# First expert network: low parts of weights and row builds moved to VectorE, sign multiplications to ScalarE

## The chip, the cores and the metric

One core of one Trainium2 chip runs the whole kernel. The metric is device time of one launch in microseconds (us). Five engines run side by side, each through its own list of instructions in order: PE (TensorE, matrix products, with PEld for its weight loads), DVE (VectorE), ACT (ScalarE), POOL (GpSimd, which here also issues all transfers that go by a list of rows) and SP (SyncE, which issues most other transfers). They wait for each other by semaphores.

## The reference

```
X = fft(fft(x, axis=1), axis=2).real          # x: 8 x 3072 x 256
x = X.reshape(N, 256)                         # N tokens
# first network (moe): soft weights
P = exp(x @ w_gate - max)
for _ in range(8):                            # Sinkhorn turns
    P /= P.sum(1) + 1e-9 ; P /= P.sum(0) + 1e-9 ; P *= N / E
for e in range(8):
    out += P[:, e:e+1] * (relu(x @ w1[e]) @ w2[e])      # w1: 256x1024, w2: 1024x256
# second network (moe2): each token goes to its best expert alone
for e in range(8):
    rows = argmax(out @ w_gate2) == e
    out2[rows] = gate_w[rows] * (relu(out[rows] @ u1[e]) @ u2[e])
```

The logits are so far apart that most tokens have one expert with any weight. So the kernel makes lists of (token, expert) pairs, gathers the rows of a list, and runs them in tiles of 128 rows.

## The kernel before

Four phases follow each other: the Fourier transform (0 to about 230 us), the lists of the first network, the first network (272 to 506 us), the lists of the second (`route2`, 506 to 535 us), and the second network (535 to 722 us).

**Tiles.** Each of the 8 experts has three fixed tiles of 128 rows. Six more, the free tiles, go to any expert that has more rows; their weights are gathered by an indirect transfer (`fw`, `rawc`, `gd`) and a free tile runs within an expert from expert 2 on.

**Products.** A float32 product is made as three products of rounded parts (float32r): high by high, low by high, high by low. For this each weight piece is split: ACT copies it to the high part (`w1h`, `w2h`, L826) and `eng` subtracts (L827, 128x1024; L830, 128x32, for eight gate columns that go with a w2 piece). `part(..., i, ...)` with i = 0, 1 are the halves of w1, with i = 2, 3 the halves of w2; in the lists below i = 4, 5 are the two halves of a free tile's w2. The hidden rows are split as well: ACT takes the relu of a PSUM tile (`hh`, L873), DVE makes `hl` from PSUM and `hh` (L434).

**Rows.** A gathered row group `Xg` (128 partitions x 3 tiles x 281) holds a row of the half spectrum; `build` makes from it the group `x` of full rows in four steps: a, the middle column added to and taken from the even part (two operations, 128x99 and 128x96); b, the mirrored part times a sign per row (128x381, `Xg<-Xg,Rsg`); c, a copy of two columns and a sum (128x381); d, a difference (128x381). PE then transposes `x` (L840, or L867 for free tiles), ACT and DVE split it into `xh` and `xl`. Groups 8 and 9 are the rows of the free tiles.

**Sinkhorn.** `sinkhorn` runs the weights of all pairs on DVE while experts 1 to 4 run: logits, `start`, eight turns of ten small DVE operations with one PE product of column sums (L984) between two turns, then `end`, which copies the weights of fixed tiles, one expert at a time, in eight copies (`Rwt<-P`).

**Order.** Nothing is scheduled: each engine's order is that of the code, and `Slots` places side work between the matrix products: slots 0 to 7 after the eight row groups of h, 8 to 10 in the free tile, 11 after the next transposition, 12 to 20 in the fixed tiles. Tables say which slot and which engine: `ONP` lists the (expert, i) whose subtraction POOL makes, `ONB` the experts in which POOL builds the next expert's rows, `FBUILD` the expert, the slots and a flag (1: POOL) for groups 8 and 9. `UPART` has the four slots of expert 7 in which the second network's first weights (u, expert 0) are split, the last two (w2 halves) on POOL. POOL also issues the weighted rows' scatter-adds to `acc` (L803, `acc<-y`), the free tiles' weight gathers, and, once `route2` has the list `Rgidx`, the gathers of the second network's rows (`Xg<-acc,Rgidx`).

```
for s, i, g in ((UPART[0], 0, V), (UPART[1], 1, V), (UPART[2], 2, G), (UPART[3], 3, G)):
    sl.at(E - 1, s, lambda i=i, g=g: part("u", 0, i, g))
on = lambda e: lambda i: G if (e, i) in ONP else V
onb = lambda e: G if e in ONB else V
```

V is VectorE, G is GpSimd. After a second half is split, `part` fetches the next weights into the buffer on SP's queue.

Of the kernel before, what the change touches and what calls it, by code (L numbers as in the profile page):

```python
# [11 lines left out]
AF = mybir.ActivationFunctionType  # L12
ALU = mybir.AluOpType
# [9 lines left out]
def fft_phase(tc, ctx, A, H, Zd, L, rmx, ident, zb, each):  # L23
# [19 lines left out]
    # gate columns in the basis of the transformed rows  # L43
# [16 lines left out]
    def warm(n):  # L60
        """keeps the tensor engine's clock up while it waits."""
        p = pp.tile([128, 512], F32, name="pp")
        for _ in range(n):
            nc.tensor.matmul(p, zb[:, :128], zb, start=True, stop=True)
# [58 lines left out]
    def logits(hd, t0, n, np_):  # L123
# [4 lines left out]
        if t0 % 12 in (0, 4) and n == 4:  # L128
            # rows that are their own mirror count once
            nc.gpsimd.memset(L[0:1, t0 + t0 % 12 // 2, 1], -3e38)  # L130
# [47 lines left out]
    def d_tiles(b, j, ps=None):  # L178
        """third j of the rows of batch b."""
# [11 lines left out]
    # the middle column of all batches  # L191
# [34 lines left out]
    def zero(i):  # L226
        """second batch, while the first is transformed."""
# [66 lines left out]
def _consts():  # L294
# [36 lines left out]
    # rows in turn: columns added, columns subtracted  # L331
# [16 lines left out]
def host_layout(inp):  # L348
# [9 lines left out]
    # rows of the gate, and those of the mirrored columns, in halves  # L358
# [7 lines left out]
NSL = 40                    # row slots per partition  # L366
NS2 = 8                     # rows with more than one live expert
NSA = NSL + 3 * NS2         # pairs: first, second, third and fourth live expert
CAP = 3                     # fixed tiles per expert
NFLAT = 6                   # tiles that any expert may take  # L370
# [3 lines left out]
DG = D + 8                  # a row and its second gate  # L374
DW = DG + 1                 # and its place in the output
# [39 lines left out]
def row_tile(t):  # L415
    """where the rows of a tile lie: after rows of no token come the free tiles."""
    return t + 1 + NFLAT if t < E * CAP else t - E * CAP + 1

# [24 lines left out]
class Route:  # L443
    """lists of rows by expert: one-hot products put every marked slot at its place."""
# [8 lines left out]
    def positions(self, T, M, n, rst, hook=lambda: None, S=None, n1=None):  # L453
        """places of the marked (expert, slot), summed over the experts; 0 for empty slots.
        The caller adds the start of the expert's tiles. Slots from n1 on come first."""
# [25 lines left out]
        # two chains in turn: tiles past the fixed ones, places  # L481
# [16 lines left out]
        if two:  # L498
            # more than a tile of other pairs
# [8 lines left out]
        def later():  # L508
            """experts of the free tiles, rows of their weights, too many tiles."""
# [17 lines left out]
    def split(self, T, gp, cs, n, nm):  # L527
        """tile and row of the places gp + cs; rounding to whole numbers by a large one."""
# [32 lines left out]
def route1(nc, rt, L, rmx, K, R, keep, pool, ring, hooks):  # L561
# [6 lines left out]
    # global maximum  # L568
# [13 lines left out]
    # a key per row: its column and the set of its live experts  # L582
# [19 lines left out]
    # one live expert of every row: the first  # L602
# [15 lines left out]
    # rows with more: their other experts in turn  # L618
# [21 lines left out]
    def during():  # L640
        # while the counts are summed: columns of the slots, first tiles of their experts
# [20 lines left out]
    # the other pairs come first, as they are asked for again  # L662
# [21 lines left out]
    def signs():  # L684
        # sign, whether the pair is the row's first
# [8 lines left out]
        # place of the row's first pair, for its other pairs  # L694
# [17 lines left out]
    def targets():  # L712
        # rows that the other pairs are added to; all else goes to rows of no token
# [23 lines left out]
def route2(nc, rt, lg, K, R, pool, ring, arrive, more, counts, warm):  # L737
# [12 lines left out]
    def choose(a, b):  # L750
        # the first expert with the largest logit
# [35 lines left out]
    # empty places take a row of no token  # L787
# [19 lines left out]
class Moe:  # L807
    """expert networks over tiles of 128 rows; float32 products as three of float32r parts."""
# [6 lines left out]
    def part(self, r, i, eng, g=None):  # L815
        """hi and lo part of a piece; g: eight more columns per row of w2."""
# [16 lines left out]
    def turn(self, xs, hook=None):  # L833
        """transpose tiles into hi and lo parts; hook: rows come tile by tile."""
# [27 lines left out]
    def free_turn(self, xs, x):  # L862
        """transpose the rows of free tiles."""
# [13 lines left out]
    def first(self, W, x, after):  # L877
        """h = relu(x w1), as hi and lo parts."""
# [13 lines left out]
    def gates(self, W, h, n, rows):  # L892
        """second gates of n tiles without their rows; h(m): hi and lo part of rows m."""
# [16 lines left out]
    def second(self, W, h, nd, after=lambda i: None):  # L910
        """h w2 for a tile; h(m): hi and lo part of rows m."""
# [14 lines left out]
    def free_first(self, w, x, i):  # L926
        """the same for a free tile, from whole float32 weights, in three steps."""
# [12 lines left out]
def boltz(nc, o, P, g, bias):  # L940
    """exp(P) as float32 has it, times 2^64: below 2^-126 in steps of 2^-149."""
# [8 lines left out]
def sinkhorn(nc, K, R, pt, pool):  # L950
    """weights of the pairs, in steps: logits of three tiles, turns, end."""
# [21 lines left out]
    def rows(it):  # L973
        o.red(rs, P, ALU.add)
        o.ts(rs, rs, 1e-9 * (2.0 ** 64 if it == 0 else 1.0), ALU.add)
# [15 lines left out]
    def end():  # L991
# [3 lines left out]
        for e in range(E):  # L995
            o.cp(R["wt"][:, e * CAP:(e + 1) * CAP], P[:, e * CAP:(e + 1) * CAP, e])
# [14 lines left out]
def dense(tc, ctx, A, K, rt, R, Ld, H, Pd, out, wg2):  # L1011
    """every row through every expert: any number of live pairs."""
# [43 lines left out]
    def network(w1, w2, xT, wt, acc):  # L1056
        """acc[tok, s] = sum over e of wt[tok, s, e] * relu(x w1) w2."""
# [67 lines left out]
# order in which weights are fetched, and the buffers they take  # L1125
# [4 lines left out]
HOLD = [("u", 0, 1)]        # after it no weights are fetched  # L1130
F0 = 2                      # first expert that a free tile goes with


def run(tc, ctx, A, out, H, acc, Ld, Pd, Gd, Zd):
# [29 lines left out]
    def zeros(n, zt=zt):  # L1164
        """output rows stay zero unless they are written later."""
# [14 lines left out]
    def fetch():  # L1180
        if order:
            s, e, b = order.pop(0)
            if b in "12":
                # room that parts of the first weights do not need yet
# [12 lines left out]
    with tc.manual_schedule():  # L1197
# [27 lines left out]
        with ExitStack() as st:  # L1225
# [7 lines left out]
            def gates2(e, qs=(0, 1)):  # L1233
                """w2 times the second gate."""
# [537 lines left out]
```

## Time and profile before

| | us |
|---|---|
| time, median of 3 runs (775.53 to 784.99) | 777.13 |
| span of the profiled execution, first to last instruction | 722.5 |
| between the two (launch and end, outside the span) | 54.6 |
| PE busy, share of the span | 635.4 (88%) |
| DVE busy | 448.1 (62%) |
| ACT busy | 340.4 (47%) |
| POOL busy | 315.4 (44%) |
| mean granted TensorE clock | 0.943 |

The profiled execution's own device time is not given beside its span; the 54.6 us are taken as outside it. A row of a timeline reads: start, duration, engine, line, operation, output<-inputs, shapes, and in brackets how long the engine was idle before it and what ended that. Durations of one engine's successive instructions overlap by about 0.1 us. A duration runs from the instruction's start to its end, so an instruction that is held up in the middle of its execution shows as a long one, not as an idle engine.

### The profile page before, as it was taken

The page shows a single profiled execution, that of the slowest core. Times are in us where ns is not written, and L with a number is a line of the kernel's source. Part 1 is how long each engine was busy: PE and PEld are TensorE (multiplying, and loading weights), DVE is VectorE, ACT ScalarE, POOL GpSimd, SP SyncE. Part 2 cuts the span into 40 slices and gives each one's busy share as a digit, 9 for nine tenths or more (in the row PEclk, how much of TensorE's full clock was granted, in tenths as well). Part 3 has the DMA queues.
Part 4 walks back from the last instruction along what each step waited for, and adds up shares of the span by engine and source line. Part 5 has one row for each costly group of instructions (what it writes and reads, how often), then busy time and mean ns, then how long its engine had stood idle before and what let it go on. Part 6 is the DMA issues. An engine that isn't in the chain of part 4 may idle for free. (4 is left out here: it accounts for less than half of the span.)

```text
span 722.5 us, 12560 instructions
## 1 busy us (share of the span) xinstructions
PE 635.4 (88%) x4749; PEld 609.5 (84%) x4749; DVE 448.1 (62%) x932; ACT 340.4 (47%) x660; POOL 315.4 (44%) x325
## 2 busy tenths in 40 slices
PE   7888978898998499896969698988499999999996
PEld 4778978898998499895959598987369999999996
DVE  3587456646347967779696946842935567556650
ACT  2455666566754204553344353653215556455651
POOL 2377446645010537839152525424347463422232
PEclk9899999999999859998879899999799999999998
DMA  8989999997769517987543478684727475467410
GB/s 223 241 225 319 325 295 280 301 303 235 258 222 358 205 41 244 197 352 246 159 154 117 151 225 236 184 310 94 250 67 252 169 271 180 164 242 252 168 56 33
DMA packets 67039, 155.43 MB, mean 215 GB/s; under 512 B 17891, under 2 KB 35787, under 8 KB 59164
## 3 DMA queue, kind: packets, MB, share of 16 engines
q1 hardware_dynamic: 56844, 114.83, 50.3%
q0 software_dynamic: 9840, 39.45, 17.3%
q8 instruction: 39, 0.64, 0.4%
q10 hardware_dynamic: 288, 0.27, 0.1%
q14 instruction: 28, 0.23, 0.1%
HBM read 104.00 MB, written 50.44 MB: 214 GB/s over the span
## 5 line engine op out<-in xcount | busy, mean ns | idle before, releaser
L920 PE MATMUL py<-w2l,hh 128*128 128x264 f32 (+1 forms) x480 | 141.5, 295 | 13.8 <-DVE w2l L830 7.8
L920 PE MATMUL py<-w2h,hh 128*128 128x264 f32 (+1 forms) x480 | 143.1, 298 | 0.0
L434 DVE SCALAR_TENSOR_TENSOR hl<-ph,hh 128x384 fp32r<-128x384 f32 (+1 forms) x164 | 85.5, 540 | 92.6 <-ACT hh L873 92.4
L920 PE MATMUL py<-w2h,hl 128*128 128x264 f32 (+1 forms) x480 | 141.2, 294 | 0.0
L920 PEld LDWEIGHTS py<-w2l,hh 128*128 128x128 f32 x480 | 95.9, 200 | 15.1 <-DVE w2l L830 8.4
L873 ACT ACTIVATE hh<-ph 128x384 fp32r<-128x384 f32 (+1 forms) x164 | 76.7, 481 | 53.6 <-PE ph L887 27.6
L150 POOL TENSOR_TENSOR xa<-xa,xm 96x1024 f32<-96x1024 f32 (+1 forms) x30 | 75.3, 2524 | 52.2 <-DMA xm<-in_xm_dram 51.5
L920 PEld LDWEIGHTS py<-w2h,hl 128*128 128x128 f32 x480 | 95.7, 199 | 0.3
L920 PEld LDWEIGHTS py<-w2h,hh 128*128 128x128 f32 x480 | 95.8, 200 | 0.1
L803 POOL DMA_INDIRECT out_dram<-y,Rorow x30 | 32.1, 1070 | 90.0 <-ACT y L1705 39.9
L887 PE MATMUL ph<-xh,w1h 128*128 128x384 f32 x256 | 67.4, 344 | 4.0 <-DVE hl L434 3.9
L73 PEld LDWEIGHTS pp<-ca,w 96*128 96x128 f32 x512 | 60.2, 196 | 6.2 <-DVE w L159 4.2
L73 PE MATMUL pp<-ca,w 96*128 96x96 f32 x512 | 61.8, 280 | 4.1 <-DVE w L159 4.1
L887 PE MATMUL ph<-xl,w1h 128*128 128x384 f32 x256 | 65.2, 336 | 0.0
L887 PE MATMUL ph<-xh,w1l 128*128 128x384 f32 x256 | 65.2, 336 | 0.0
L75 ACT ACTIVATE at<-pp 128x384 f32<-128x384 f32 x64 | 54.0, 847 | 21.1 <-PE pp L73 19.5
L90 PE MATMUL pp<-cb,t 128*128 128x128 f32 x368 | 49.3, 279 | 11.4 <-DVE t L83 11.4
L90 PEld LDWEIGHTS pp<-cb,t 128*128 128x128 f32 x368 | 45.4, 194 | 12.5 <-DVE t L83 12.5
L887 PEld LDWEIGHTS ph<-xh,w1h 128*128 128x128 f32 x256 | 45.0, 188 | 6.6 <-DVE hl L434 5.2
L83 DVE COPY t<-pp 128x512 f32<-128x512 f32 (+2 forms) x56 | 32.4, 608 | 24.6 <-PE pp L81 24.6
L119 DVE COPY hd<-pp 128x281 f32<-128x281 f32 x32 | 14.3, 448 | 53.3 <-ACT hd L121 35.0
L887 PEld LDWEIGHTS ph<-xl,w1h 128*128 128x128 f32 x256 | 46.3, 188 | 0.1
(335 smaller groups left out, 1336.2 us busy)
## 6 DMA issues: line engine op xcount, KB each, us to landing
out_dram<-zt SPq DMA_DIRECT2D x48, 512.0 KB, 3.0
H<-hd SPq DMA_DIRECT2D x24, 562.0 KB, 6.4
xa<-in_xa_dram SPq DMA_DIRECT2D x32, 384.0 KB, 6.1
xm<-in_xm_dram SPq DMA_DIRECT2D x32, 384.0 KB, 8.8
rawa<-in_w_dram SPq DMA_DIRECT2D x8, 1024.0 KB, 6.4
rawb<-in_w_dram SPq DMA_DIRECT2D x8, 1024.0 KB, 8.3
rawa<-in_u_dram SPq DMA_DIRECT2D x8, 1024.0 KB
rawb<-in_u_dram SPq DMA_DIRECT2D x8, 1024.0 KB, 6.1
```

Source lines behind the costliest of these rows:

```text
L73: nc.tensor.matmul(p[:M, i], lhs(4 * h + i), ca, start=True, stop=True)
L75: nc.scalar.activation(out=at[:M, :, :, s0:s0 + 4].rearrange("m g j s -> m s g j"), in_=p[:M], func=AF.Copy)
L83: nc.vector.tensor_copy(out=t[:, :n, :M], in_=p[:, :n, :M])
L90: nc.tensor.matmul(p[:M, i * 128:(i + 1) * 128], t[:, i, :M], cb[:, (g0 + i) * 128:(g0 + i + 1) * 128], start=True, stop=True)
L119: nc.vector.tensor_copy(out=hd, in_=p[:n, :HW])
L150: e.tensor_tensor(out=xa[:, c], in0=xa[:, c], in1=xm[:, c], op=ALU.add)
L434: self.nc.vector.scalar_tensor_tensor(out, a, s, b, op0, op1)
L803: nc.gpsimd.indirect_dma_start(out=dst, out_offset=bass.IndirectOffsetOnAxis(ap=idx, axis=0), in_=src, in_offset=None, **kw)
L873: self.nc.scalar.activation(out=a[:, :n], in_=p[:, :n], func=AF.Relu)
L887: self.nc.tensor.matmul(p[:, :N], w, xx, start=(i == 0), stop=(i == 5))
L920: self.nc.tensor.matmul(p[:, :nd], c, W[2 + m // 4][w][:, m % 4, :nd], start=(m == 0 and i == 0), stop=(m == 7 and i == 2))
```

## The change

Low parts of the first network that POOL subtracted are subtracted by DVE, 14 pieces; POOL's three row builds go to DVE as well (groups of experts 3 and 4, and group 8); the sign multiplication of every build goes to ACT, as three operations of 128x127 with a scale per row in place of one of 128x381; the two w2 pieces of the second network's expert 0 leave slots 15 and 16 of expert 7 and come after `route2` and the gathers' issue, their subtraction on DVE; two small Sinkhorn operations take another form. Transfers of SP keep their order. Comments that were dropped are not shown.

```
-        o.ts(rs, rs, 1e-9 * (2.0 ** 64 if it == 0 else 1.0), ALU.add)
+        o.stt(rs, rs, 1e-9 * (2.0 ** 64 if it == 0 else 1.0), rs, ALU.add, ALU.bypass)
...
-        for e in range(E):
-            o.cp(R["wt"][:, e * CAP:(e + 1) * CAP], P[:, e * CAP:(e + 1) * CAP, e])
+        own = P.rearrange("p t e -> p (t e)")[:, :E * (8 * CAP + 1)].rearrange("p (e x) -> p e x", e=E)[:, :, 0:8 * CAP:8]
+        o.stt(R["wt"][:, :E * CAP].rearrange("p (e c) -> p e c", e=E), own, 1.0, own, ALU.mult, ALU.bypass)
...
                     grab2(j)
                 assert zat[0] == 97
+                for i in (2, 3):
+                    part("u", 0, i, nc.vector)
                 xt = moe.turn(lambda i: X[0][:, i], lambda i: warm(3))
...
-UPART = (7, 11, 15, 16)
-ONP, ONQ, ONB = [(2, 0), (2, 1), (2, 2), (2, 3), (3, 0), (3, 1), (3, 2), (3, 3), (4, 0), (4, 1), (4, 3), (4, 4), (5, 4), (7, 4)], [(7, 5)], (2, 3)
+UPART = (7, 11)
+ONP, ONQ, ONB = [], [(7, 5)], ()
...
-FBUILD = ((1, (11, 12, 14, 15), 1), (4, (11, 12, 12, 15), 0))
+FBUILD = ((1, (11, 12, 14, 15), 0), (4, (11, 12, 12, 15), 0))
...
         def b():
-            tt(X[j][:, t, 137:264], X[j][:, t, 137:264], R["sg"][:, s, None].to_broadcast([128, n, 127]), ALU.mult)
+            for k in range(a0, a0 + n):
+                v = X[j][:, k, 137:264]
+                nc.scalar.activation(out=v, in_=v, func=AF.Copy, scale=R["sg"][:, CAP * j + k:CAP * j + k + 1])
...
-    for s, i, g in ((UPART[0], 0, V), (UPART[1], 1, V), (UPART[2], 2, G), (UPART[3], 3, G)):
-        sl.at(E - 1, s, lambda i=i, g=g: part("u", 0, i, g))
+    for s, i in ((UPART[0], 0), (UPART[1], 1)):
+        sl.at(E - 1, s, lambda i=i: part("u", 0, i, V))
```

**DVE at the end of expert 1.** Before, from the last `hl` of the expert's h to the split of expert 2's rows (`Xg_2707` is group 8, `Xg_2731` group 9, `sg_`, `P` the logits of Sinkhorn):

```order
L434 SCALAR_TENSOR_TENSOR hl_3282<-ph_3274,hh_3281 128x384
L827 TENSOR_TENSOR w1l_3286<-rawa_3066,w1h_3285 128x1024
L425 TENSOR_TENSOR sg__2970<-Xg_2707 128x24
L425 TENSOR_TENSOR P_2969<-Xg_2707,Rsg_83 128x24
L425 TENSOR_TENSOR P_2969<-P_2969,sg__2970 128x24
L425 TENSOR_TENSOR sg__2970<-Xg_2731 128x24
L425 TENSOR_TENSOR P_2969<-Xg_2731,Rsg_83 128x24
L425 TENSOR_TENSOR P_2969<-P_2969,sg__2970 128x24
L827 TENSOR_TENSOR w1l_3319<-rawa_3066,w1h_3318 128x1024
L425 TENSOR_TENSOR xl_3377<-pt_3378,xh_3376 128x384
```

With the change the same stretch reads:

```order
L434 SCALAR_TENSOR_TENSOR hl_3286<-ph_3278,hh_3285 128x384
L827 TENSOR_TENSOR w1l_3290<-rawa_3068,w1h_3289 128x1024
L1550 TENSOR_TENSOR Xg_2707<-Xg_2707 128x3x33
L1550 TENSOR_TENSOR Xg_2707<-Xg_2707 128x3x32
L425 TENSOR_TENSOR sg__2970<-Xg_2707 128x24
...
L425 TENSOR_TENSOR sg__2970<-Xg_2731 128x24
L425 TENSOR_TENSOR P_2969<-Xg_2731,Rsg_83 128x24
L425 TENSOR_TENSOR P_2969<-P_2969,sg__2970 128x24
L827 TENSOR_TENSOR w1l_3325<-rawa_3068,w1h_3324 128x1024
L1565 COPY Xg_3336<-Xg_2707 128x3x2
L1550 TENSOR_TENSOR Xg_3336<-Xg_2707 128x3x127 x2
```

Steps c and d of group 8 (the last two rows) stand behind the logits of group 9 and a w1 subtraction; before, POOL made them from its own queue.

**DVE in expert 2.** Before, a Sinkhorn turn's last operations, the second half of the free tile's w2, and the `hl` of the expert's h:

```order
L425 TENSOR_TENSOR pr<-P,rp 128x240
L440 TENSOR_REDUCE cs<-pr 128x8
L425 TENSOR_TENSOR P<-P,ri 128x240
L827 TENSOR_TENSOR w2l<-rawc,w2h 128x4x256
L830 TENSOR_TENSOR w2l<-gd,w2h 128x4x8
L434 SCALAR_TENSOR_TENSOR hl<-ph,hh 128x384 x4
L431 TENSOR_SCALAR cs<-pt 128x8
```

With the change, from the same turn to the next one's start:

```order
L440 TENSOR_REDUCE cs<-pr 128x8
L425 TENSOR_TENSOR P<-P,ri 128x240
L827 TENSOR_TENSOR w2l<-rawb,w2h 128x4x256
L830 TENSOR_TENSOR w2l<-g_76,w2h 128x4x8
L827 TENSOR_TENSOR w2l<-rawb,w2h 128x4x256
L830 TENSOR_TENSOR w2l<-g_76,w2h 128x4x8
L827 TENSOR_TENSOR w2l<-rawc,w2h 128x4x256
L830 TENSOR_TENSOR w2l<-gd,w2h 128x4x8
L434 SCALAR_TENSOR_TENSOR hl<-ph,hh 128x384
L1550 TENSOR_TENSOR x<-Xg 128x3x127
L434 SCALAR_TENSOR_TENSOR hl<-ph,hh 128x384 x3
L827 TENSOR_TENSOR w1l<-rawa,w1h 128x1024
```

The two halves of w2 (`rawb`), a build step and a half of w1 have joined DVE's queue; POOL had them.

**DVE around the second lists.** Before, the list `Rgidx` is followed at once by the split of the gathered rows:

```order
L434 SCALAR_TENSOR_TENSOR d<-pt,e__5525 128x30
L425 TENSOR_TENSOR Rgidx<-pt,d 128x30
L425 TENSOR_TENSOR xl<-pt,xh 128x384 x2
L429 TENSOR_SCALAR nf<-inb 128x1
L425 TENSOR_TENSOR Rovf<-Rovf,nf 128x1
```

With the change:

```order
L434 SCALAR_TENSOR_TENSOR d<-pt,e__5524 128x30
L425 TENSOR_TENSOR Rgidx<-pt,d 128x30
L827 TENSOR_TENSOR w2l<-rawb,w2h 128x4x256 x2
L425 TENSOR_TENSOR xl<-pt,xh 128x384 x2
L429 TENSOR_SCALAR nf<-inb 128x1
```

The two subtractions of (u, expert 0) now run on DVE while POOL issues the gathers that `Rgidx` releases; before, POOL made them some 20 us earlier.

## Rows read from the trace of the kernel before

**Rows 1.** Busy time by stretch (the view of windows): experts 2, 3, 4 and 5, then from the end of expert 6's h to the logits of the second network, and an expert of the second network. Columns: stretch and its length, then busy us and (instructions) of PE, PEld, DVE, ACT and POOL, the granted TensorE clock, the DMA engines' share, GB/s.
```profile
314.90:352.70 37.80, 30.09 (x192) 29.41 (x191) 32.54 (x64) 13.36 (x27) 18.01 (x18) 0.86 0.76 273
352.70:387.30 34.60, 27.76 (x190) 27.18 (x189) 28.79 (x51) 13.55 (x27) 12.94 (x11) 0.85 0.48 148
387.30:421.60 34.30, 27.50 (x193) 26.97 (x192) 26.00 (x52) 14.32 (x29) 13.43 (x12) 0.90 0.49 160
421.60:450.80 29.20, 25.92 (x184) 25.66 (x183) 18.54 (x33) 13.68 (x27) 14.74 (x9) 0.94 0.70 208
475.00:506.50 31.50, 26.78 (x180) 24.52 (x178) 11.76 (x22) 15.60 (x28) 9.13 (x10) 0.95 0.65 175
572.00:596.00 24.00, 24.00 (x185) 24.00 (x184) 14.13 (x25) 13.28 (x24) 12.82 (x12) 1.00 0.60 216
```

**Rows 2.** The list of waits over the whole span, three of those in which PE waits for DVE: total us, how often, the longest.
```profile
PE pt L466 <- DVE cd L440: 11.8, 2, 10.0
...
PE pt L984 <- DVE cs L440: 8.7, 2, 6.3
...
PE py L920 <- DVE w2l L830: 7.8, 3, 6.1
```

**Rows 3.** The timeline of PE in expert 2, a wait between two Sinkhorn turns, and two successive products behind it.
```profile
343.72 0.60 PE L984 MATMUL pt<-cs,tri 128*128 128x8 f32 x2 [4.53 <-DVE xl L425]
...
345.19 0.42 PE L920 MATMUL py<-w2l,hh 128*128 128x264 f32 x1
345.41 0.42 PE L920 MATMUL py<-w2h,hl 128*128 128x264 f32 x1
```

**Rows 4.** The timeline of DVE: small operations in experts 2 (first two rows, the first and the last of four alike), 3 (three rows) and 4 (the eight copies of `end`), and in the second network's lists (two rows).
```profile
325.22 1.83 DVE L429 TENSOR_SCALAR rs<-rs 128x30 f32<-128x30 f32 x1
...
337.93 2.35 DVE L429 TENSOR_SCALAR rs<-rs 128x30 f32<-128x30 f32 x1
...
364.70 7.84 DVE L429 TENSOR_SCALAR rs<-rs 128x30 f32<-128x30 f32 x1
...
377.12 0.18 DVE L429 TENSOR_SCALAR rs<-rs 128x30 f32<-128x30 f32 x1
...
378.89 2.29 DVE L425 TENSOR_TENSOR P<-P,ri 128x240 f32<-128x240 f32 x1
...
400.79 8.31 DVE L437 COPY Rwt<-P 128x3 f32<-128x3 f32 x8
...
508.00 5.75 DVE L425 TENSOR_TENSOR kp<-big,km 128x22 f32<-128x22 f32 x1
...
515.38 0.17 DVE L425 TENSOR_TENSOR kp<-big,km 128x8 f32<-128x8 f32 x1
```

**Rows 5.** The timeline of POOL at the same times.
```profile
365.06 2.43 POOL L827 TENSOR_TENSOR w2l<-rawb,w2h 128x1024 fp32r<-128x1024 f32 x1
...
370.13 2.35 POOL L827 TENSOR_TENSOR w1l<-rawa,w1h 128x1024 fp32r<-128x1024 f32 x1
...
406.59 2.33 POOL L827 TENSOR_TENSOR w1l<-rawa,w1h 128x1024 fp32r<-128x1024 f32 x1
...
508.48 5.21 POOL L827 TENSOR_TENSOR w2l<-rawb,w2h 128x1024 fp32r<-128x1024 f32 x2
```

**Rows 6.** Groups of instructions by line and shape, 271.6 to 535 us: count, busy us, mean ns of one, idle time before them.
```profile
L827 DVE TENSOR_TENSOR w1l<-rawa,w1h 128x1024 fp32r<-128x1024 f32 x10 | 12.1, 1215 | 0.0
...
L1547 DVE TENSOR_TENSOR x<-Xg 128x381 f32<-128x381 f32 x10 | 5.5, 547 | 0.0
...
L829 ACT ACTIVATE w2h<-g 128x32 fp32r<-128x32 f32 x14 | 3.1, 222 | 0.0
...
L873 ACT ACTIVATE hh<-ph 128x256 fp32r<-128x256 f32 x6 | 2.3, 384 | 2.4 <-PE ph L933 2.4
...
L830 DVE TENSOR_TENSOR w2l<-g,w2h 128x32 fp32r<-128x32 f32 x9 | 1.7, 193 | 0.0
...
L1547 DVE TENSOR_TENSOR Xg<-Xg 128x99 f32<-128x99 f32 x6 | 1.5, 250 | 0.0
```

**Rows 7.** The end of expert 1: DVE (the first logits operation of group 9, whose last gathered rows end its wait, and the subtraction behind the logits) and PE (the first transposition of group 8).
```profile
310.36 0.41 DVE L425 TENSOR_TENSOR sg__2970<-Xg 128x24 f32<-128x24 f32 x1 [2.78 <-DMA Xg<-H,Rhidx]
...
311.78 1.21 DVE L827 TENSOR_TENSOR w1l<-rawa,w1h 128x1024 fp32r<-128x1024 f32 x1
...
309.47 0.55 PE L867 MATMUL pt<-ident,Xg 128*128 128x128 f32 x3 [0.28 <-POOL Xg L1547]
```

**Rows 8.** POOL in experts 5 and 7, a subtraction each for a free tile, and PE's wait at the second of them.
```profile
433.82 2.94 POOL L827 TENSOR_TENSOR w2l<-rawc,w2h 128x1024 fp32r<-128x1024 f32 x1
...
495.36 2.92 POOL L827 TENSOR_TENSOR w2l<-rawc,w2h 128x1024 fp32r<-128x1024 f32 x1
...
498.54 0.39 PE L920 MATMUL py<-w2l,hh 128*128 128x264 f32 x1 [2.71 <-POOL y L1588]
```

**Rows 9.** POOL's gathers, by list `Rhidx` during expert 0 and 1 and by `Rgidx` at the start of the second network, and the DVE subtraction that runs beside the second row.
```profile
288.73 1.41 POOL L798 DMA_INDIRECT Xg<-H,Rhidx  x1 [0.31 <-issue]
...
300.86 1.86 POOL L798 DMA_INDIRECT Xg<-H,Rhidx  x1 [0.30 <-DVE x L1547]
...
528.97 1.01 POOL L798 DMA_INDIRECT Xg<-acc,Rgidx  x1 [15.27 <-DVE Rgidx L425]
...
300.58 1.22 DVE L827 TENSOR_TENSOR w2l<-rawb,w2h 128x1024 fp32r<-128x1024 f32 x1
```

More of the change, by code (lines that the diff above doesn't have):

```diff
@@ L1544, in build @@
     def build(j, eng, i=None):
-        a, n = (0, CAP) if i is None else (i, 1)
-        s, t = slice(CAP * j + a, CAP * j + a + n), slice(a, a + n)
+        a0, n = (0, CAP) if i is None else (i, 1)
+        t = slice(a0, a0 + n)
         tt = lambda out, a, b, op: eng.tensor_tensor(out=out, in0=a, in1=b, op=op)
```

## The prediction

> **What bounds the kernel now.** I read the busy time by stretch first. An expert of undisturbed products takes 24.0 us at a granted clock of 1.00; experts 2 to 5 take 37.8, 34.6, 34.3 and 29.2 us [rows 1], and in all of them the clock is below 1. PE is busy 27.5 to 30.1 us of the first three, so each loses 4 to 8 us to waits and 3 to 6 us to slower products. The list of waits says who is late: DVE, in the column sums between Sinkhorn turns (8.7 us over two waits), in a w2 low part (7.8 us), and in the second network's lists (11.8 us) [rows 2]. PE's timeline shows the second loss: behind a wait of 4.53 us successive products stand 0.22 us apart [rows 3], the lower of the clock's two levels (1.2 of 2.4 GHz).
>
> So DVE's own rows come next. Operations of 30 elements a partition, 0.18 us elsewhere, last 1.83, 2.35 and 7.84 us; eight tiny copies last 8.31 us; one of 22 elements lasts 5.75 us [rows 4]. Beside them POOL runs its subtractions, 2.3 to 2.6 us each: three of them in a row from 365.06 to 372.48, and DVE's 7.84 us end at 372.54; three until 408.92, and the copies end at 409.10; two until 513.69, and the 5.75 us end at 513.75 [rows 4, 5]. DVE is not short of time in these stretches, it is held until POOL's run of subtractions ends. Operations that read PSUM (`hl`) do not show it. That is why I take the stretch as POOL's doing and as returned when POOL stops subtracting.
>
> **The change part by part.** First the stretch. Expert 2 has four such operations, 1.83, 2.14, 2.85 and 2.35 us instead of 0.18 to 0.41, 8.2 us over; expert 3 two, 7.66 and 1.88 over; expert 4 the copies, 7.6 over [rows 4]. Against this stands what DVE gets. A w subtraction is 1.22 us on DVE, a gate piece 0.19, step a 0.50, each half of c and d 0.55, the copy 0.15 [rows 6]. Expert 2 gets four subtractions, two gate pieces and a build without its sign step: 4.9 + 0.4 + 1.75 = 7.0 us. Expert 3 gets the same, expert 4 four subtractions and two gate pieces, 5.3 us. DVE's busy time becomes:
>
> - expert 2: 32.5 - 8.2 + 7.0 = 31.3 us, above PE's 24.0, so DVE sets the stretch. It was idle 5.3 us in this one; I leave it a quarter: **32.5** instead of 37.8 us, **-5.3**.
> - expert 3: 28.8 - 9.5 + 7.0 = 26.3, with 0.7 idle **27** instead of 34.6, **-7.6**.
> - expert 4: 26.0 - 7.6 + 5.3 less some 0.6 for eight copies that become one = 23.1, below PE. PE's 24.0 and 2.5 for small waits: **26.5** instead of 34.3, **-7.8**.
>
> Expert 5 to the logits of the second network, 421.6 to 506.5 us: two POOL subtractions of 2.9 us go, one of them ahead of a PE wait of 2.71 us [rows 8]. But POOL's scatter-adds to `acc` follow each other there and each waits for the one before to land, and this chain, not PE, ends at the logits. I take half of the two, **-3** (0 to -7).
>
> The second network's lists: `kp` 5.75 becomes 0.17, with PE waiting 10.0 us at its end [rows 2, 4]: **-5.6**. The two subtractions move behind `Rgidx`, which releases the gathers. A gather takes 1.01 us there, and 1.41 and 1.86 when a DVE subtraction runs beside it; the 1.86 end at 302.72, 0.9 after that subtraction [rows 9]. The first gathers would run beside two of 1.22 us: **+0.9** (0 to 2.0, the two cut by their overlap). The subtraction moved also holds back the next 1 MB fetch, which now runs beside the gathers: **+0.6** (0 to 1.5). Both w2 pieces are needed only when the 8 row groups of h are done, some 8 us after the rows arrive, so the pieces themselves are covered.
>
> The Trainium skill, page "SBUF — State Buffer", section "Who interferes with whom", has the holding of [rows 4, 5] as an exclusive lock on a port pair that DVE and GpSimd share, and adds that a DVE operation with two SBUF inputs takes only the read side, which descriptor generation (what a gather does on GpSimd) does not need. By that the gathers would not be held at all and the sum would be 0.9 us lower; the rows of 1.41 and 1.86 us speak against it here.
>
> The end of expert 1 gets worse. DVE waits until 310.36 for the last gathered rows [rows 7], makes the logits of group 9 (0.5 us without POOL beside them), then a w1 subtraction of 1.22, and only then, in the new order, the copy and steps c and d of group 8 (0.15 + 2 x 0.55): c is ready at about 312.7 and d at 313.2. PE wanted c at 309.47 [rows 7], so it starts 3.2 us later, and a stop of this size has slowed the products behind it [rows 3]: **+4** (3 to 5).
>
> The sign steps: 30 ACT operations, each between the 0.22 us of 32 elements and the 0.38 of 256 [rows 6], near 0.3. Three per build are 0.9 us on an engine busy 13 to 16 us per expert [rows 1]; step c on DVE now waits for them, and one to three slots lie between. I count **0**. Without that cover a build would cost 0.9 us on DVE's path, some 3 us over experts 2 to 4. "ScalarE: Activation LUTs" of the Trainium skill, section "🎯 Rules for kernel authors", says the opposite of this edit: multiplications belong on VectorE. Here DVE is the engine that is late, so what each costs alone (0.9 against about 0.6) does not decide.
>
> Sum: +4 - 5.3 - 7.6 - 7.8 - 3 - 5.6 + 0.9 + 0.6 = -23.8 us, on a span of 722.5: 698.7. The 54.6 us outside stay, so 777.1 - 23.8 = **753 us**.
>
> **The rivals.**
>
> *Larger gain.* DVE loses all its idle time and PE all slow products: expert 2 at 29.8, 3 at 25, 4 at 24.5 (-8, -9.6, -9.8), the scatter chain moves with PE (-7), `kp` -5.6, the end of expert 1 at 0: -40.0, **737 us**. For it speaks that each wait costs twice, as a wait and as clock; against it, that DVE's 31.3 us in expert 2 exceed PE's work.
>
> *Smaller gain: DVE keeps the waits that it has.* If idle times remain as they were (5.3, 5.8, 8.3 us), the experts take 36.6, 32.1 and 31.4: -1.2, -2.5, -2.9; with +4, -5.6, +1.5 and -1 for the scatter chain it is -7.7, **769 us**. It would come through the products L984, which need all of a turn: three subtractions in a row now stand between one turn and the next `hl`. Against it: the idle time in [rows 1] came mostly behind stretched operations, since PE had stopped and sent DVE nothing.
>
> *Slower.* The stretch is not POOL's doing, or is paid again with DVE holding POOL, and the moved work comes on top: 7.0 + 7.0 + 5.3 us in experts 2 to 4, +4 and +1.5 = +24.8, **802 us**. With a share r of the stretch returned (25.3 us in the experts, 5.6 in `kp`) and nothing covered, the change is 24.8 - 30.9 r: over +15.5 only for r below 0.3, no gain below 0.8. Against it stand the three ends that agree within 0.2 us.
>
> *The change doesn't do what it says.* POOL keeps one subtraction, in the second network, and its issue work; nothing of the first network's subtractions stays there. I give it nothing.
>
> **How the numbers follow.** The forecast gets 0.62, the larger gain 0.14, the smaller 0.16, the slower 0.08. A measurement of this kernel can tell about 2%, 15.5 us: below 761.6 is faster, above 792.7 slower. The forecast's own terms (-3 to -9.5 in expert 3, 0 to -7 in the scatter chain) give it 744 to 762. Faster: all of the larger gain, nearly all of the forecast (0.60) and a quarter of the smaller (0.04), 0.78. Slower: over half of its rival, 0.05. Same: 0.17. The range leaves out the far half of the larger gain and most of the slower case: 739 to 769.
>
> **What would show it.** Right: no DVE operation of 30 elements over 0.5 us in experts 2 to 4; `kp` at 0.2 us; expert 3 near 27 us and clock 0.95 or more; PE's first transposition of group 8 waiting 3 us for DVE; a first gather after `Rgidx` of 1.4 us or more. Wrong: experts 2 and 3 still over 33 us with DVE busy all through, waits of `hl` behind the three w2 subtractions, an ACT wait at step c, or logits (`lg<-acc`) that come no earlier than PE's gain allows because a scatter-add is on the way.

## The result, and the profile after

The changed kernel takes 759.41 us (median of 4 runs, 749.42 to 762.59), the kernel before 777.23 us: -17.8 us, a ratio of 0.9665 with a 95% interval of 0.9572 to 0.9759. Two of the changed kernel's four runs (762.36 and 762.59) were in a slower state, at a clock of 0.90 instead of 0.92, and the ratio leaves them out, so it stands for -26 us (19 to 33) and not for -17.8. The forecast was 753 us, 739 to 769.

The two profiles can't be set side by side by their spans. The one with the change has 754.7 us, close below its own time of 756.46; the one of before had 722.5, far below every run of before. So nearly all of the 54.6 us that I took as lying outside the span lies inside it in the runs that were timed. The largest single piece shows in the trace. The first row is POOL's last gather of the first network's rows, the second PE, in the middle of the first transpositions (columns as before):

```profile
308.88 0.95 POOL L798 DMA_INDIRECT Xg<-H,Rhidx  x1 [0.30 <-issue]
...
314.92 1.01 PE L1260 MATMUL py<-zb 128*128 128x512 bf16 x2 [30.35 <-remote]
```

PE stands still for 30.35 us, on a filler product that waits for nothing but PE's own earlier product, and goes on 6.0 us after the last gather was issued. "remote" means that the trace shows nothing that ended the wait. The profile of before has no such wait. It comes back below; here it means that only stages can be compared.

**The stages.** The view of windows for experts 1 to 6, from the h of expert 7 to the list products, and from there to the second network:

```profile
335.50:355.80 20.30, 19.42 (x135) 18.49 (x134) 14.94 (x43) 12.94 (x28) 0.00 (x0) 1.00 0.89 228
355.80:387.20 31.40, 27.41 (x192) 26.41 (x191) 28.76 (x73) 14.20 (x30) 2.97 (x5) 0.95 0.63 221
387.20:418.40 31.20, 26.58 (x191) 26.34 (x190) 25.48 (x62) 14.21 (x30) 2.97 (x5) 0.95 0.56 178
418.40:444.80 26.40, 25.26 (x193) 25.05 (x192) 20.45 (x49) 15.88 (x35) 5.04 (x6) 1.00 0.67 224
444.80:468.90 24.10, 24.10 (x184) 24.10 (x183) 16.58 (x34) 14.35 (x30) 10.37 (x6) 1.00 0.69 203
468.90:493.10 24.20, 24.20 (x185) 24.20 (x184) 14.96 (x28) 14.35 (x30) 3.63 (x4) 1.00 0.88 260
493.10:536.40 43.30, 26.13 (x181) 24.83 (x180) 16.93 (x40) 15.83 (x28) 15.67 (x14) 0.85 0.62 171
536.40:559.50 23.10, 18.20 (x96) 12.83 (x99) 11.21 (x31) 4.29 (x6) 6.53 (x6) 0.80 0.48 153
```

Against [rows 1] experts 2 to 5 fall from 135.9 to 113.1 us, POOL is nearly idle in experts 2 and 3 (2.97 us each instead of 18.01 and 12.94), and the clock is 0.95 or more. Then the gain stops: expert 7 to the list products takes 43.3 us, and the lists take 23.1; in the profile of before they took 41.3 and 19.0.

**DVE's small operations.** The timeline of DVE, one operation each of experts 2 and 3 and of the lists, and three rows of its queue in expert 3:

```profile
366.96 0.19 DVE L434 SCALAR_TENSOR_TENSOR rs<-rs 128x30 f32<-128x30 f32 x1
...
400.21 0.19 DVE L434 SCALAR_TENSOR_TENSOR rs<-rs 128x30 f32<-128x30 f32 x1
...
402.79 1.22 DVE L827 TENSOR_TENSOR w2l<-rawb,w2h 128x1024 fp32r<-128x1024 f32 x1
...
404.02 1.22 DVE L827 TENSOR_TENSOR w2l<-rawb,w2h 128x1024 fp32r<-128x1024 f32 x1
...
405.73 1.22 DVE L827 TENSOR_TENSOR w1l<-rawa,w1h 128x1024 fp32r<-128x1024 f32 x1
...
407.33 0.15 DVE L431 TENSOR_SCALAR cs<-pt 128x8 f32<-128x8 f32 x1
...
533.55 0.21 DVE L425 TENSOR_TENSOR kp<-big,km 128x22 f32<-128x22 f32 x1
```

What lasted 1.83 to 7.84 us in [rows 4] lasts 0.19, and `kp` 0.21 instead of 5.75.

**PE's waits.** PE's timeline in expert 3, in the h of expert 7, and at the list products, and ACT's in expert 7:

```profile
407.54 0.90 PE L840 MATMUL pt<-ident,x 128*128 128x128 f32 x3 [4.62 <-DVE cs L431]
...
509.07 0.69 PE L887 MATMUL ph<-xh,w1h 128*128 128x384 f32 x1 [10.61 <-DVE hl L434]
...
536.36 0.19 PE L466 MATMUL pt<-cd,trib 128*128 128x8 bf16 x1 [6.56 <-DVE cd L440]
...
506.13 1.06 ACT L826 ACTIVATE w2h<-rawc 128x1024 fp32r<-128x1024 f32 x1 [11.30 <-DMA rawc<-in_w_dram,Rfrow]
```

The second has grown: at this place PE waits 1.70 us in the profile of before, and 6.30 us in a later one of the same kernel (experiment 1). PE needs `hl` from DVE, DVE needs `hh` from ACT, and ACT stands 11.30 us at the copy of a free tile's weight whose gather has not landed; the relus are queued behind it. That gather was issued late, because POOL's queue has a run of scatter-adds ahead of it, each waiting:

```profile
475.02 1.58 POOL L803 DMA_INDIRECT acc<-y,Rapos  x1 [9.28 <-DVE hl L434]
...
483.40 1.90 POOL L803 DMA_INDIRECT acc<-y,Roidx  x1 [6.66 <-DMA acc<-y]
493.85 1.55 POOL L803 DMA_INDIRECT acc<-y,Rapos  x1 [8.55 <-issue]
495.70 1.01 POOL L798 DMA_INDIRECT fw<-in_w_dram,Rfrow  x1 [0.30 <-PE ph L887]
497.02 0.97 POOL L798 DMA_INDIRECT rawc<-in_w_dram,Rfrow  x1 [0.30 <-issue]
```

**Behind the second lists**, POOL's first gather and DVE beside it (timeline), then what the chain of waits puts ahead of PE's second transposition:

```profile
549.11 1.76 POOL L798 DMA_INDIRECT Xg<-acc,Rgidx  x1 [14.02 <-DVE Rgidx L425]
...
548.75 2.35 DVE L827 TENSOR_TENSOR w2l<-rawb,w2h 128x1024 fp32r<-128x1024 f32 x2
...
551.17 5.19 DMA Xg<-acc,Rgidx
```

The gather takes 1.76 us instead of 1.01 [rows 9], and the second one's data land 5.19 us after its issue. SP issues the fetch of the next weights (`rawb` from u) at 551.13, beside them.

### The profile page after: what moved, and what is told of

Read it like the earlier page. It is cut to its first block, busy times and chain, and to the rows that moved or that the text cites. A ratio compares the mean times of both kernels' runs of the same rounds, so it can differ in the third digit from the quotient of the medians.

```text
span 754.7 us, 12554 instructions
## 1 busy us (share of the span) xinstructions
PE 644.0 (85%) x4745; PEld 619.0 (82%) x4749; DVE 427.4 (57%) x955; ACT 348.7 (46%) x690; POOL 258.7 (34%) x283
## 5 line engine op out<-in xcount | busy, mean ns | idle before, releaser
L920 PE MATMUL py<-w2l,hh 128*128 128x264 f32 (+1 forms) x480 | 138.6, 289 | 4.2 <-DVE w2l L830 3.1
L920 PE MATMUL py<-w2h,hh 128*128 128x264 f32 (+1 forms) x480 | 140.6, 293 | 1.8 <-issue 1.8
L920 PE MATMUL py<-w2h,hl 128*128 128x264 f32 (+1 forms) x480 | 138.1, 288 | 0.2
L920 PEld LDWEIGHTS py<-w2l,hh 128*128 128x128 f32 x480 | 93.1, 194 | 5.3 <-DVE w2l L830 3.3
L920 PEld LDWEIGHTS py<-w2h,hh 128*128 128x128 f32 x480 | 93.1, 194 | 2.3 <-issue 2.2
L920 PEld LDWEIGHTS py<-w2h,hl 128*128 128x128 f32 x480 | 93.0, 194 | 0.4 <-issue 0.3
L73 PEld LDWEIGHTS pp<-ca,w 96*128 96x128 f32 x512 | 63.7, 205 | 6.2 <-DVE w L159 4.7
L73 PE MATMUL pp<-ca,w 96*128 96x96 f32 x512 | 64.3, 286 | 4.8 <-DVE w L159 4.8
L75 ACT ACTIVATE at<-pp 128x384 f32<-128x384 f32 x64 | 54.1, 848 | 24.1 <-PE pp L73 22.4
L887 PEld LDWEIGHTS ph<-xh,w1l 128*128 128x128 f32 x256 | 47.4, 192 | 0.0
```

Source lines behind the costliest of these rows:

```text
L73: nc.tensor.matmul(p[:M, i], lhs(4 * h + i), ca, start=True, stop=True)
L75: nc.scalar.activation(out=at[:M, :, :, s0:s0 + 4].rearrange("m g j s -> m s g j"), in_=p[:M], func=AF.Copy)
L887: self.nc.tensor.matmul(p[:, :N], w, xx, start=(i == 0), stop=(i == 5))
L920: self.nc.tensor.matmul(p[:, :nd], c, W[2 + m // 4][w][:, m % 4, :nd], start=(m == 0 and i == 0), stop=(m == 7 and i == 2))
```

## The experiments

Three chips ran these experiments. Chip 7 (experiments 2 and 3, and the first two profiles of 1) runs the kernel before in 740.3 us (13 runs), chip 6 (experiment 4) in 780.9 and chip 10 (the last profile of 1, and experiments 5 and 6) in 783.6 us (7 runs each). Ratios are to before on the same chip. Which chip ran the pair of the result is not recorded.

**1. The kernel before again, twice, and the changed one again.** No edit.

> The kernel before, profiled again, because the execution with the change has a PE wait of 30.35 us at the start of the first network (284.4 to 314.92 us, two transpositions after its first one) that no engine of the trace ends, and because its span lies only 1.8 us below its own time while the 722.5 us of before lie 55 us below the median of before. Theory S1, the wait belongs to both kernels in most executions and the profiled one of before had none: span within 3 us of the time, about 770 to 780 us, with a PE wait of 25 us or more between 255 and 320 us. Theory S2, the wait comes with the change (its three sign operations on ACT ahead of the first rows): span 720 to 728 us, no PE wait over 12 us between 255 and 320 us.

> The changed kernel, profiled again. Theory S1 (a wait that comes and goes with the execution): span 715 to 760 us, the wait at the start of the first network of another size or gone; experts 2 to 5 at 113 us in sum within 3 us either way. Theory S2 (a cost of the change): the wait is there again, 28 to 33 us.

> The kernel before once more. Where the changed kernel shows the wait of 30 us at the start of the first network on this chip: theory (the wait is the chip's, in every kernel), a wait of 25 to 45 us between 255 and 325 us here too and a span of 770 to 785 us; rival (only kernels with the sign step on ACT have it), no such wait. Where the chip does not show it: span 732 to 745 us and no wait over 12 us there.

On chip 7 neither kernel has the wait: before 741.33 us (span 739.6), changed 724.67 (span 722.9), one run each. On chip 10 the kernel before has it too, with the same end, 6.0 us after its last gather's issue at 310.13 (PE's timeline):

```profile
316.15 1.01 PE L1259 MATMUL py<-zb 128*128 128x512 bf16 x2 [27.23 <-remote]
```

So the wait goes with the chip and not with the change (S1, with the chip in the place of the execution), and the time is the span plus 1.8 us. The growing wait in the h of expert 7 is there too:

```profile
531.67 0.69 PE L887 MATMUL ph<-xh,w1h 128*128 128x384 f32 x1 [6.30 <-DVE hl L434]
```

Stages in us, each from PE's first product of it to the next's; "with" and "without" speak of the wait at the start. The columns are one profile each: before on chip 10, the profile after, and before and changed on chip 7.

| | before, with | changed, with | change | before, without | changed, without | change | forecast |
|---|---|---|---|---|---|---|---|
| expert 1 | 23.1 | 20.3 | -2.8 | 24.9 | 28.8 | +3.9 | +4 |
| expert 2 | 37.9 | 31.4 | -6.5 | 36.1 | 31.5 | -4.6 | -5.3 |
| expert 3 | 34.7 | 31.1 | -3.6 | 34.6 | 31.7 | -2.9 | -7.6 |
| expert 4 | 34.3 | 26.4 | -7.9 | 34.3 | 26.4 | -7.9 | -7.8 |
| experts 5 and 6 | 53.4 | 48.3 | -5.1 | 53.4 | 48.3 | -5.1 | |
| expert 7 to list products | 46.2 | 43.3 | -2.9 | 41.8 | 45.4 | +3.6 | |
| sum of the last two | 99.7 | 91.6 | -8.1 | 95.2 | 93.7 | -1.5 | -8.6 |
| lists to the second network | 19.8 | 23.2 | +3.4 | 18.8 | 24.5 | +5.7 | +1.5 |
| expert 1 to the second network | 249.5 | 224.0 | -25.5 | 243.9 | 236.7 | -7.2 | -23.8 |

Without the wait the stages that the change touches gain only 7.2 us, though the span is 16.7 us shorter. 11.0 us of that lie ahead of the first network's list products, where the two kernels have the same code (PE's first list product, before and then changed, both on chip 7):

```profile
250.09 0.17 PE L466 MATMUL pt<-cd,trib 128*128 128x8 bf16 x1 [1.81 <-DVE cd L440]
...
239.06 0.17 PE L466 MATMUL pt<-cd,trib 128*128 128x8 bf16 x1 [1.82 <-DVE cd L440]
```

That part is a difference between executions and not of the change: in experiments 2 and 3 on the same chip this product starts at 242.7 and 239.7.

Without the wait, the new order at the end of expert 1 stops PE, in the timeline of the changed kernel on chip 7:

```profile
319.28 1.51 PE L867 MATMUL pt<-ident,Xg 128*128 128x128 f32 x6 [5.29 <-DVE Xg L1550]
```

With the wait PE stops 0.76 us there: the last gather is issued 6.0 us before PE goes on, and DVE does not wait for its rows.

**2. The subtractions alone.**

```
-ONP, ONQ, ONB = [(2, 0), (2, 1), ... (7, 4)], [(7, 5)], (2, 3)     # before
+ONP, ONQ, ONB = [], [(7, 5)], (2, 3)
```

> The kernel before with one edit: the 14 subtractions of the first network go from POOL to DVE; the row builds stay on POOL, the sign step on DVE, the second network's two pieces in slots 15 and 16 on POOL. Theory of the prediction (POOL's subtractions hold DVE, the time comes back when they go): small DVE operations of Sinkhorn return to 0.2 to 0.4 us, except beside a build step of POOL (at most 1.2 us); experts 2 to 5 fall from 135.9 to 113 to 119 us; kp stays at 4 to 6 us; time 17 to 23 us below before, less the share of a start wait. Rival (DVE's own work becomes the bound): experts 2 to 4 together above 100 us, time within 8 us of before.

717.46 us (4 runs), ratio 0.9685 (0.9585 to 0.9786): as much as the whole change has (0.9665 in the result, 0.9696 on chip 6), from this one table. On this chip the rest of the change costs: the one run of the changed kernel (724.67) lies above all four of these (711.89 to 720.47), and its expert 1 and its lists are 5.5 and 5.2 us longer. Experts 2 to 5 take 32.0, 30.3, 27.6 and 24.3 us, 114.2 in sum. The Sinkhorn operations are short though they keep their old form, so the new form is not what shortened them (DVE's timeline in experts 2, 3 and 4):

```profile
326.04 0.18 DVE L429 TENSOR_SCALAR rs<-rs 128x30 f32<-128x30 f32 x1
...
367.58 0.36 DVE L429 TENSOR_SCALAR rs<-rs 128x30 f32<-128x30 f32 x1
...
398.74 0.65 DVE L437 COPY Rwt<-P 128x3 f32<-128x3 f32 x8
```

`kp` is short, yet the stretch beside the lists is not gone; it has moved on to the operation that now meets POOL's two pieces (DVE's and POOL's timelines):

```profile
499.84 0.18 DVE L425 TENSOR_TENSOR kp<-big,km 128x22 f32<-128x22 f32 x1
...
500.44 5.59 DVE L425 TENSOR_TENSOR lg<-lg,y 128x8 f32<-128x8 f32 x1
...
500.78 5.21 POOL L827 TENSOR_TENSOR w2l<-rawb,w2h 128x1024 fp32r<-128x1024 f32 x2
```

DVE's operation of 8 elements ends at 506.03, POOL's run at 505.99. So what is stretched depends on when POOL runs. It depends on the kind of operation too: in the kernel before a TENSOR_REDUCE inside POOL's subtraction keeps its usual time, and the TENSOR_SCALAR behind it is held to the end (DVE's timeline, then POOL's):

```profile
324.78 0.41 DVE L440 TENSOR_REDUCE rs<-P 128x30 f32<-128x240 f32 x1
325.22 1.83 DVE L429 TENSOR_SCALAR rs<-rs 128x30 f32<-128x30 f32 x1
...
324.43 2.59 POOL L827 TENSOR_TENSOR w2l<-rawb,w2h 128x1024 fp32r<-128x1024 f32 x1 [10.41 <-ACT w2h L826]
```

The other three profiles with the old engines (the kernel before twice, and experiment 3) have the same pair, 0.40 and 1.83 to 1.84 us.

**3. The two pieces behind the lists alone.** The change's edit of `UPART`, its loop and the two lines in `run`, on the kernel before.

> The kernel before with one edit: the two w2 pieces of the second network's first expert move behind the second lists and onto DVE. Theory of the prediction: kp falls from 5.75 to 0.2 us, PE's wait at the list products from 10.0 to 4.5 us, the first gather behind the list takes 1.4 to 2.0 us instead of 1.0; time 3 to 5 us below before. Rival (the gathers or the fetch behind them give it back): from the list to the first product of the second network's h 2 us longer or more, time within 2 us of before.

734.52 us (10 runs), ratio 0.9906 (0.9856 to 0.9955). `kp` takes 0.18 us, the first gather 1.75, PE's wait at the list products is 6.13 us; from there to the second network it is 22.2 us instead of 18.8. The net of 5.6 gained and 3.4 given back is 2.2, a little under the 3.3 to 10.7 us of the interval; one profile doesn't say where the rest is.

**4. The changed kernel on chip 6, and its parts.**

> The changed kernel beside the next three, on the same chip and the same runs of before. By the look above (722.9 us of span, no wait at the start of the first network): time 0.965 to 0.985 of before; PE stopped about 5 us at the first transposition of group 8, about 12 us in the h of expert 7, about 7 us at the list products.

757.32 us, ratio 0.9696 (0.9625 to 0.9767). The start wait is there (29.85 us), so the stop at group 8 is not; 9.79 us in the h of expert 7, 7.51 at the list products.

```
-FBUILD = ((1, (11, 12, 14, 15), 0), (4, (11, 12, 12, 15), 0))
+FBUILD = ((1, (11, 12, 14, 15), 1), (4, (11, 12, 12, 15), 0))
```

> The changed kernel with one edit undone: the rows of group 8 are built by POOL again. Theory of the prediction (steps c and d of group 8 stand on DVE behind the logits of group 9, which wait for the last gathered rows): the stop of 5.3 us at the first transposition of group 8 falls below 1 us, expert 1 from 28.9 to 23 to 25 us; time 3 to 6 us below the changed kernel. Rival (what expert 1 gains is lost again at the scatter-adds, which set the end of the network): expert 1 shorter by 4 us or more, the lists' start no more than 1 us earlier relative to the network's start.

757.18 us, 0.9727 (0.9658 to 0.9795). Inconclusive for its question: on this chip the start wait hides the stop, and expert 1 only goes from 20.3 to 19.2 us. The 28.8 us of the changed kernel on chip 7 stand beside 23.3 us of the run with the subtractions alone there, which builds group 8 on POOL but differs in the other builds and the sign steps too.

```
-UPART = (7, 11)
+UPART = (7, 11, 15, 16)
-                for i in (2, 3):
-                    part("u", 0, i, nc.vector)
-    for s, i in ((UPART[0], 0), (UPART[1], 1)):
-        sl.at(E - 1, s, lambda i=i: part("u", 0, i, V))
+    for i, s in enumerate(UPART):
+        sl.at(E - 1, s, lambda i=i: part("u", 0, i, V))
```

> The changed kernel with one edit altered: the two w2 pieces of the second network go back to slots 15 and 16 of expert 7, but their subtraction stays on DVE. Theory (the move behind the list costs by itself, the first gather is held and the fetch runs beside the gathers; POOL's subtraction was the only harm in the old place): first gather 1.0 instead of 1.75 us, from the list products to the second network's first h 24.5 down to 19 to 21 us, kp stays at 0.2 us; time 3 to 5.5 us below the changed kernel. Rival (the pieces in slots 15 and 16 delay the last rows of the first network, as ACT copies them first): the list products start 2 us later or more, time within 2 us of the changed kernel.

749.65 us (5 runs), 0.9615 (0.9553 to 0.9677); the interval overlaps that of the changed kernel, so the gain of the old place rests on the stages. POOL's first gather takes 1.02 us again and the lists 19.3 us instead of 24.1; `kp` stays at 0.18. The long `kp` needed another engine and not another place (POOL's timeline):

```profile
550.67 1.02 POOL L798 DMA_INDIRECT Xg<-acc,Rgidx  x1 [15.91 <-DVE Rgidx L425]
```

```
-  (3, 3, 7, 13, 0, 2)],      # "w", expert 7
+  (3, 3, 7, 13, 11, 12)],
```

> The changed kernel with one edit: in expert 7 the split of the free tile's gathered w2 moves from slots 0 and 2 to slots 11 and 12, behind the h of the expert (the last expert runs its free tile behind its first fixed tile). Theory A (ACT's copy of a late gathered weight holds the relus queued behind it on ACT, and PE with them): the wait of about 12 us in the h of expert 7 falls below 2 us, the lists start 6 to 10 us earlier, time 5 to 10 us below the changed kernel. Theory B (the chain of scatter-adds, each waiting for the one before to land, sets the end of the network whatever PE does): the wait in h goes, but PE's wait at the list products grows by nearly as much, and the time stays within 3 us.

755.82 us, 0.9724 (0.9641 to 0.9807). The wait in the h of expert 7 is gone, and PE has it again at the list products (PE's timeline):

```profile
533.78 0.19 PE L466 MATMUL pt<-cd,trib 128*128 128x8 bf16 x1 [18.67 <-DVE cd L440]
```

From expert 7's start to there it is 43.5 us, as it was (42.9 and 43.3). This is theory B: it is not PE that sets the end of the first network but what leads to its logits. The chain of waits of this run goes back from the logits' read over two scatter-adds, and 12 of these follow each other from 439.16 to 521.99.

**5. What paces the scatter-adds.**

```
-ZERO = [..., (4, 11, 16), (4, 11, 16), (2, 11), (2, 11), (2, 11), (2,)]
+ZERO = [..., (4, 7, 11, 14, 16), (2, 4, 7, 11, 14, 16), (2,), (2,), (), ()]
```

> The changed kernel with one edit: of the writes of zeros to the output (0.5 MB a pair) seven that were queued in experts 4 to 7 are queued in experts 2 and 3 instead. Theory (the scatter-adds set the end of the first network, and what slows each is the load on the DMA engines beside it): from expert 2's start to the list products 173 to 178 us instead of 181 to 183; time 3 to 8 us below the changed kernel. Rival (each scatter-add takes its time whatever runs beside it, or the load is that of the weights alone): 180 to 184 us, time the same within 2 us.

754.62 us, 0.9675 (0.9613 to 0.9737). Expert 7 to the list products goes from 42.9 to 39.1 us, from expert 2's start it is 177.5 instead of 181.6. The time is not told apart from that of the changed kernel (757.32 on chip 6, ranges overlap). From the first to the last issue of the 12 scatter-adds it is 78.2 us instead of 82.1, and 74.8 and 75.9 in the two kernels of experiment 6, which have the same edit and the late split. That speaks for the load on the DMA engines as one part of the chain's pace; each is one profile.

**6. Joined.** Group 8 on POOL, the two pieces in slots 15 and 16 on DVE, the free tile's split late, the zeros early; and the same without builds and sign steps on the new engines.

> The changed kernel with four edits joined: group 8 built by POOL, the second network's two w2 pieces in slots 15 and 16 with the subtraction on DVE, the free tile's split in expert 7 behind its h, and the writes of zeros queued in experts 2 and 3. Theory: list products to the second network's h 19 to 20 us instead of 24; no wait over 2 us in the h of expert 7; first transposition of group 8 without a stop; time 0.945 to 0.96 of before. Rival (the scatter-adds hold the end of the first network): list products no earlier than in the changed kernel, time 0.958 to 0.967 of before.

> The kernel before with the 14 subtractions and the second network's two on DVE in their old slots, the free tile's split in expert 7 behind its h, and the writes of zeros queued in experts 2 and 3; the row builds stay on POOL and the sign step is not on ACT. Theory (the subtractions were all of the harm, the builds and the sign step bring little): within 4 us of the joined kernel beside it. Rival (builds and sign step matter as DVE is the engine that is late): 5 us or more slower than it.

The first takes 744.08 us (4 runs, 740.47 to 752.01), ratio 0.9527 (0.9436 to 0.9617), the lowest ratio of all that ran; lists 19.9 us, 38.3 us from expert 7 to the list products, where PE still waits 14.38 us. The second takes 749.81 us (749.0 to 751.8), 0.9625 (0.9567 to 0.9683). In the two profiles the difference sits in expert 1 (23.2 against 19.2 us) and expert 4 (27.7 against 26.4), and is given back in part in expert 3 (30.4 against 31.2). By these stages builds on DVE and signs on ACT are worth some 4 us; the times differ by 5.7 us, but the intervals overlap, so they don't decide between the two expectations.

## Why the prediction was right, and where its terms were off

**The stretch is POOL's, and comes back: right.** The run with the subtractions alone shows it by itself: without POOL's subtractions the Sinkhorn operations are short in their old form, experts 2 to 5 take 114.2 us, and where POOL still subtracts, DVE's next operation waits to the end of the run. The slower rival needed less than 0.3 of the stretch returned; experts 2 and 4 came out within 1.2 us of their terms.

**Expert 3, -7.6: mis-sized, -3.6 and -2.9.** I let DVE's idle time fall from 5.8 to 0.7 us "since PE had stopped and sent DVE nothing". It is still 5.7 us (31.20 less 25.48). Here the rival "DVE keeps the waits that it has" was right: two w2 pieces and a w1 piece stand between a turn's end and the next read of the column sums at 407.33, and PE's transposition at 407.54 waits 4.62 us for that read. PE, busy 26.58 us, has this one wait in the expert, and the two make up the 31.20 us. The price was right, the cover was not.

**The end of expert 1, +4: the right wait where its condition held, the size by luck.** On the chip without the start wait it is +3.9, but the stop is 5.29 us and not the 3.2 that I took, and the 24.9 us it is measured against have a wait of 1.52 us for `fw` that the profile of before had not: against its 23.1 it is +5.7. With the start wait DVE does not wait for the gathered rows, and expert 1 gains 2.8 us.

**From expert 5 to the logits, -3 (0 to -7): the chain was right, the gain is not shown.** From expert 5's start to DVE's read of the logits it is 89.7 us before and 87.3 after with the start wait (-2.4), 85.4 and 89.4 without (+4.0). Neither is clear of the spread: the kernel before has 85.0 us in its first profile, and 89.3 in experiment 3, which leaves its experts as they were. Experts 5 and 6 gain 5.1 us in both, and expert 7 gives back some or all of it. I had named the chain of scatter-adds and still counted half of POOL's two subtractions as gain; the run with the free tile's split late shows that such a wait of PE is worth nothing there, since the list products don't move when one of 10 us goes. The chain is no shorter for faster experts: its 12 scatter-adds are issued over 81.9 us before and 82.6 after with the wait, 78.2 and 84.3 without. So a sign that I had named for being wrong came: logits that come no earlier because a scatter-add is on the way.

**`kp`, -5.6: right** (0.21 us). **The gathers, +0.9: right** (1.76 against 1.01, +0.75), and the run with the pieces in slots 15 and 16 takes it away by their place alone. Here the measurement and the Trainium skill (page "SBUF — State Buffer", section "Who interferes with whom") part: the page infers that a DVE operation with two SBUF inputs leaves descriptor generation alone; the seven profiles with the pieces there have 1.75 to 1.76 us, the seven without 1.01 to 1.02. **The fetch behind them, +0.6: too small.** The gathered rows that PE waits for land 5.19 us after their issue instead of 2.77, and the lists lose 3.4 to 5.7 us in all; the runs move the split and the fetch together and don't tell them apart. So the edit took 5.6 us and gave most of it back, for a move that the run with the pieces in slots 15 and 16 shows to be needless.

**The sign steps, 0: as forecast.** They take 0.40 us each instead of the 0.3 that I took. No step c waits for one in the profile after; on chip 7 that of the very first rows does, 4.29 us, but from the first network's list products to its first h product it is 40.1 us there and 39.8 before. The last two runs speak for some gain from them and the builds together. The group of the sign steps by line and shape in that profile, 284 to 536 us:

```profile
L1560 ACT ACTIVATE Xg<-Xg,Rsg 128x127 f32<-128x127 f32 x27 | 8.8, 396 | 0.0
```

**The time itself** is right in part by luck, as terms missed to both sides: expert 3 by +4, expert 5 to the logits by up to +7, the lists by +2 to +4, expert 1 by -7 or nothing. With the start wait they cancel, -25.5 us against the -23.8 that I added up; without it, the condition of the profile that I read, they don't, -7.2. And the step "the 54.6 us outside stay" was wrong in its reason: 1.8 us lie outside. The later profile of before with the start wait is 60.3 us longer than the first: 27.2 are that wait, some 17 more lie ahead of the first expert, 6.5 in the first network and the lists behind it, and 9.5 in the second network.

## What to carry to other kernels

Where a tiny operation on VectorE lasts microseconds, look for GpSimd's work that ends at the same moment, and try that work on another engine in its old place first. Once the busy engine is relieved, price what comes next along its whole chain: the queue of scatter-adds here, each waiting for the one before, did not get shorter because the matrix products ahead of it did. And compare profiles by stages, after checking that the span and the timed run belong together.

## What the runs showed of the hardware

A small TENSOR_SCALAR or TENSOR_TENSOR of VectorE that meets GpSimd's run of subtractions lasts until that run ends: 7.84 us beside three of them, 5.75 and 5.59 beside two, with ends within 0.06 us of each other. The same kinds of operation take 0.18 to 0.36 us without them. A TENSOR_REDUCE (0.41 us) and an `hl`, which reads PSUM (0.56 us at 394.10 in the kernel before), are not held.

On chips 6 and 10, and in the profile after, PE stopped for 27 to 30 us on a product that waits for PE's own earlier one, in 9 profiles out of 9, in kernels with and without the change, each time until 5.9 to 6.3 us after the last of 30 gathers was issued; on chip 7 in none of 4, nor in the first profile of before. In the profile after the granted clock is 0.51 from 284.0 to 316.8 us, near its lower level of 1.2 GHz, as PE does next to nothing. The trace names no cause, and none was tried; a kernel that issues these gathers in two groups would tell whether the wait follows them. The rest of the difference between the chips (the first products of the second network's first expert take 24 to 27 us in the profiles with the wait and 18 in those without) stays open too.
